# Product of state and C in a Mamba-2 kernel: two products of 64 rows in two banks, one for each half of the heads

The kernel runs on one core of a Trainium2 chip (trn2). The metric is the time of one execution on the device, in microseconds (us), read as the median of several runs.

## The reference, cut to what matters

Four sequences of 768 tokens, 8 heads of width 32, state size 16, go through a chunked state-space layer; its output, 3072 x 256, goes through a feed-forward layer of width 2048. All is fp32.

```python
# per chunk of the sequence (the kernel uses chunks of 128 tokens)
M = einsum('bhin,bhjn->bhij', Cc, Bc) * L          # L: decays, lower triangle
y_intra = einsum('bhij,bhjd->bhid', M, xc)
y_inter = einsum('bhin,bhnd->bhid', Cc, state) * exp(cum)   # the product changed here
y = y_intra + y_inter
state = decay * state + sum_j(Bc x xc * decay_from_j)
...
h = y @ w_in
out = (h * cos(h)) @ w_out
```

## The kernel before

Six chunks of 128 tokens are worked off; in the feed-forward loop of one chunk (16 steps: `hp` = first product, `o` = second) the state-space work of the next chunk is threaded in, one piece in a step: `turn` (transposes), `intra` (C·B products into `g`, times decays into `m`), `finish` (state product and `m`·x into `y`, then the new state's product `s_ps`). Chunk 0 has no state, so 5 chunks x 4 sequences = 20 calls of `finish` hold the state product.

The state of one sequence is kept block-diagonal: partitions are (head, state index) = 8 x 16, columns are (head, width) = 8 x 32, and all but a head's own block is zero. Columns 0 to 127 (heads 0 to 3) are thus non-zero only in rows 0 to 63, columns 128 to 255 only in rows 64 to 127.

```python
def pair(name):                       # two banks, two such tiles in turn
    return psum.tile([P, 2, 4 * P], FP32, tag="scan", bufs=2, name=name)

def finish(c, b, tag=None, fills=0):
    (bcT, m), xr = part.pop((c, b)), raw[c][1]
    y = (pair("y")[:, 0] if tag is None else bank([P, 4 * P], "y", tag)
         ).rearrange("p (k i) -> p k i", k=4)
    fill(y[:, 2:4], fills)
    y = y[:, 0:2]
    if c > 0:
        s = state[c - 1, b].rearrange("p h d -> p (h d)")
        for t in range(2):
            PE.matmul(y[:, t], lhsT=s[:, t * P:(t + 1) * P], rhs=bcT[:, 1],
                      start=(t == 0), stop=False, skip_group_check=True)
    for h in range(H):                                  # y<-m,xr
        q, t = h % 4, h // 4
        PE.matmul(y[32 * q:32 * q + 32, t], lhsT=xr[:, b, h], rhs=m[:, h],
                  start=(c == 0 and t == 0), stop=True, tile_position=(0, 32 * q), ...)
    ...
    ACT.copy(out=yT[c][:, :, b * P:(b + 1) * P], in_=y)
    if c > 0:
        carry(c, b)                                     # s_ps<-xr,sc, 128x32 tiles

def intra(c, b):
    ...
    for u in range(4):                                  # g<-cT,bcT, 32x128 tiles
        r = slice(32 * u, 32 * u + 32)
        PE.matmul(g[u // 2][:, u % 2, 0:2 * P], lhsT=bcT[r, 0], rhs=cT[r]..., ...)
```

Of the kernel before, what the change touches and what calls it, by code (L numbers as in the profile page):

```python
# [25 lines left out]
def kernel(  # L26
# [23 lines left out]
    V, ACT, G, PE = nc.vector, nc.scalar, nc.gpsimd, nc.tensor  # L50
# [3 lines left out]
    P = 128  # L54
# [24 lines left out]
    def bank(shape, name, tag):  # L79
        return psum.tile(shape, FP32, tag=tag, bufs=2, name=name)  # L80

    def pair(name):

        return psum.tile([P, 2, 4 * P], FP32, tag="scan", bufs=2, name=name)
# [6 lines left out]
    def fill(dst, times=1):  # L91

        for _ in range(times):
            PE.matmul(dst, lhsT=ones, rhs=ones.unsqueeze(1).to_broadcast([P, dst.shape[1], P]),  # L94
                      start=True, stop=True, skip_group_check=True)
# [104 lines left out]
    for n in (0, 2, 1, 3, 4, 5):  # L200
# [14 lines left out]
                    fill=0.0, base=0, channel_multiplier=1)  # L215
    G.affine_select(out=own, in_=own, pattern=[[N, H], [0, D]], compare_op=ALU.is_ge,
                    fill=0.0, base=N - 1, channel_multiplier=-1)
# [92 lines left out]

    def finish(c, b, tag=None, fills=0):
        (bcT, m), xr = part.pop((c, b)), raw[c][1]
        y = (pair("y")[:, 0] if tag is None else bank([P, 4 * P], "y", tag)
             ).rearrange("p (k i) -> p k i", k=4)
        fill(y[:, 2:4], fills)
        y = y[:, 0:2]
        if c > 0:
            s = state[c - 1, b].rearrange("p h d -> p (h d)")
            for t in range(2):
                PE.matmul(y[:, t], lhsT=s[:, t * P:(t + 1) * P], rhs=bcT[:, 1],  # L320
                          start=(t == 0), stop=False, skip_group_check=True)
        for h in range(H):
            q, t = h % 4, h // 4
            PE.matmul(y[32 * q:32 * q + 32, t], lhsT=xr[:, b, h], rhs=m[:, h],  # L324
                      start=(c == 0 and t == 0), stop=True, tile_position=(0, 32 * q),
                      skip_group_check=True)
        if b == 0:
            yT[c] = two.tile([P, 2, TB], FP32, tag="yT", name="yT")
        ACT.copy(out=yT[c][:, :, b * P:(b + 1) * P], in_=y)  # L329
        if c > 0:  # L330
            carry(c, b)

    def carry(c, b):

        if c == NC - 1:
            return
        xr, sc = raw[c][1], scaled.pop((c, b))
        s_ps = pair("s_ps")[:, 0, 0:2 * D]
        for q in range(4):
            two_ = slice(2 * q, 2 * q + 2)  # L340
            PE.matmul(s_ps[32 * q:32 * q + 32], lhsT=sc[:, two_].rearrange("p h n -> p (h n)"),  # L341
                      rhs=xr[:, b, two_].rearrange("p h d -> p (h d)"), start=True, stop=True,
                      tile_position=(0, 32 * q), skip_group_check=True)
        state[c, b] = new = states.tile([P, H, D], FP32, tag="state", name="state")
        by_two = "p (k t) d -> p k (t d)"
        V.tensor_tensor(out=new.rearrange(by_two, k=HP),
                        in0=s_ps.unsqueeze(1).to_broadcast([P, HP, 2 * D]),
                        in1=own.rearrange(by_two, k=HP), op=ALU.mult)
        if c > 0:
            V.scalar_tensor_tensor(out=new, in0=state.pop((c - 1, b)),  # L350
                                   scalar=reach[c, b][:, P - 1:P], in1=new,
                                   op0=ALU.mult, op1=ALU.add)
# [59 lines left out]
    decays(0, 2, 1)  # L412
    turn(0, 1)
    finish(0, 0, "o")
    intra(0, 1)
    grade(*order[0])
    spread_a(3, ("o", "h"))
    decays(0, 3, 0)
    decays(0, 3, 1)
    turn(0, 2, "h")  # L420
    finish(0, 1, "o", 1)
    intra(0, 2)
    turn(0, 3, "h")
    grade(*order[2])
    join(*order[0])
    finish(0, 2, "o", 1)
    intra(0, 3)
    grade(*order[1])
# [76 lines left out]
```

## Time and profile before

| | before |
|---|---|
| time, median of 3 runs | 410.0 us (409.17 to 410.1) |
| span of the profiled run | 408.6 us |
| TensorE busy | 401.1 us, 98% |
| VectorE, ScalarE busy | 65%, 43% |
| state product | 80 matmul instructions (40 products, two passes each), 12.2 us "busy" |

TensorE is busy all the way, so the question is what TensorE's own sequence costs.

### The profile page before, as it was taken

The numbers are of one execution on the slowest core, as the hardware profiler recorded it, in microseconds if no ns is written. First come the engines' busy times: TensorE is split into PE (matmuls) and PEld (weight loads), VectorE is DVE, ScalarE is ACT, GpSimd is POOL, SyncE is SP. The second block draws the span as 40 slices with busy tenths as digits, with TensorE's granted clock in tenths as the row PEclk, the third lists the DMA queues.
The fourth block names the chain that finished last, engine by engine and source line by source line (L and its number), as shares of the span: only waits on it lengthen the run. The fifth ranks groups of instructions, "written<-read, shape, count | busy, mean of one in ns | idle before, by whom it ended". The sixth has DMA issues, their size and how long they took to land.

```text
span 408.6 us, 5540 instructions
## 1 busy us (share of the span) xinstructions
PE 401.1 (98%) x2094; PEld 263.1 (64%) x2094; DVE 266.7 (65%) x410; ACT 173.8 (43%) x329; POOL 42.3 (10%) x62
## 2 busy tenths in 40 slices
PE   8999999999999999999999999999999999999995
PEld 6646666666666666666666666666666666666664
DVE  4989999945768754777663677674566664444442
ACT  2476666534343434344334433433434342433332
POOL 2164555400000000000000000000000000000000
PEclk9999999999999999999999999999999999999999
DMA  7999994291111092110164211120100000100001
GB/s 96 327 138 309 390 177 113 62 120 54 51 52 53 0 171 63 53 43 10 51 117 65 70 34 51 53 78 0 53 1 2 0 0 2 51 0 2 0 0 53
DMA packets 105979, 30.28 MB, mean 74 GB/s; under 512 B 75168, under 2 KB 101856, under 8 KB 105952
## 3 DMA queue, kind: packets, MB, share of 16 engines
q1 hardware_dynamic: 105952, 29.92, 30.9%
q8 instruction: 16, 0.26, 0.3%
q14 instruction: 11, 0.09, 0.1%
HBM read 26.57 MB, written 3.34 MB: 73 GB/s over the span
## 4 chain that ended last, share of the span: by engine, by line
PE 97%; ACT 1%; DVE 1%; issue 0%; DVEq 0%
PE hp L361 42%; PE o L385 41%; PE g L302 4%; PE y L324 3%; PE y L320 2%; PE a_ps L251 2%; PE warm L94 1%; PE tp L283 1%; PE tp L284 1%; PE s_ps L341 1%; PE y L94 0%; ACT cT L288 0%; ACT w L372 0%; DVE m L306 0%; DVE gT L374 0%
## 5 line engine op out<-in xcount | busy, mean ns | idle before, releaser
L361 PE MATMUL hp<-yT,w_in 128*128 128x512 f32 x384 | 185.0, 604 | 0.6 <-DVE gT L374 0.6
L385 PEld LDWEIGHTS o<-w_out,gT 128*128 128x128 f32 x768 | 145.9, 190 | 59.9 <-issue 44.0
L385 PE MATMUL o<-w_out,gT 128*128 128x256 f32 x768 | 181.1, 379 | 0.0
L365 ACT ACTIVATE k<-hp 128x512 int32<-128x512 f32 x96 | 57.4, 597 | 127.2 <-PE hp L361 127.1
L374 DVE TENSOR_TENSOR gT<-hp,w 128x512 f32<-128x512 f32 x96 | 66.3, 690 | 65.4 <-ACT w L372 65.4
L367 DVE SCALAR_TENSOR_TENSOR w<-hp,k 128x512 f32<-128x512 f32 x96 | 66.0, 687 | 62.3 <-ACT k L365 60.9
L361 PEld LDWEIGHTS hp<-yT,w_in 128*128 128x128 f32 x384 | 67.8, 190 | 57.7 <-issue 53.7
L372 ACT ACTIVATE w<-w,quarter 128x512 f32<-128x512 f32 x96 | 69.3, 722 | 75.1 <-DVE w L367 75.1
L267 DVE TENSOR_TENSOR_SCAN lam<-arow,unit 128x512 f32<-128x512 f32 x40 | 48.6, 1214 | 0.0
L306 DVE TENSOR_TENSOR m<-g,lam 128x512 f32<-128x512 f32 x48 | 30.7, 681 | 0.7 <-PE g L302 0.6
L276 POOL TENSOR_TENSOR sc<-bc,lam 128x128 f32<-128x128 f32 x20 | 8.2, 412 | 203.0 <-DVE lam L267 200.6
L288 ACT ACTIVATE cT<-tp,slot 128x128 f32<-128x128 f32 x48 | 14.6, 355 | 12.7 <-PE tp L284 12.7
L302 PE MATMUL g<-cT,bcT 32*128 32x256 f32 x192 | 17.1, 426 | 1.2 <-ACT bcT L290 1.2
L324 PE MATMUL y<-m,xr 128*32 128x128 f32 x384 | 15.8, 279 | 0.2 <-DVE m L306 0.2
L191 DVE SCALAR_TENSOR_TENSOR mag<-words,mag 128x512 uint32<-128x512 uint32 x16 | 13.4, 840 | 0.6
L329 ACT COPY yT<-y 128x256 f32<-128x256 f32 x24 | 8.9, 372 | 11.3 <-PE y L324 11.3
L302 PEld LDWEIGHTS g<-cT,bcT 32*128 32x128 f32 x192 | 7.5, 182 | 8.7 <-issue 6.5
L320 PEld LDWEIGHTS y<-bcT,state 128*128 128x128 f32 x80 | 12.1, 191 | 1.0
L171 POOL TENSOR_SCALAR mag<-mag 128x512 f32<-128x512 f32 x16 | 11.7, 731 | 9.4 <-ACT mag L170 9.2
L320 PE MATMUL y<-bcT,state 128*128 128x128 f32 x80 | 12.2, 274 | 0.0
L324 PEld LDWEIGHTS y<-m,xr 128*32 128x32 f32 x384 | 8.9, 109 | 4.3 <-DVE m L306 1.4
L170 ACT ACTIVATE mag<-words 128x512 f32<-128x512 f32 x16 | 10.9, 681 | 0.9 <-DMA words<-in_moe_w_in_dram 0.9
(43 smaller groups left out, 156.0 us busy)
## 6 DMA issues: line engine op xcount, KB each, us to landing
arow<-a_cut SPq DMA_DIRECT2D x20, 512.0 KB
words<-in_moe_w_in_dram SPq DMA_DIRECT2D x8, 512.0 KB
words<-in_moe_w_out_dram SPq DMA_DIRECT2D x8, 512.0 KB
xr<-in_x_dram SPq DMA_DIRECT2D x5, 512.0 KB
out_dram<-ob SPq DMA_DIRECT2D x10, 256.0 KB
bc<-in_B_dram SPq DMA_DIRECT2D x5, 256.0 KB
bc<-in_C_dram SPq DMA_DIRECT2D x5, 256.0 KB
along<-a_all SPq DMA_DIRECT2D x20, 64.0 KB
```

The source lines that it names most:

```text
L267: V.tensor_tensor_scan(out=lam[c, b][:, hs].rearrange("p h i -> p (h i)"), data0=rows_.rearrange("p h i -> p (h i)"), data1=unit.rearrange ...
L288: ACT.activation(cT[:, t], tp[:, 1], AF.Copy, scale=slot[:, t:t + 1])
L302: PE.matmul(g[u // 2][:, u % 2, 0:2 * P], lhsT=bcT[r, 0], rhs=cT[r].rearrange("p t i -> p (t i)"), start=True, stop=True)
L306: V.tensor_tensor(out=m[:, hs].rearrange("p (k t) i -> p k (t i)", k=2), in0=g[u][:, :, 0:2 * P], in1=l[:, hs].rearrange("p (k t) i -> p k ...
L320: PE.matmul(y[:, t], lhsT=s[:, t * P:(t + 1) * P], rhs=bcT[:, 1], start=(t == 0), stop=False, skip_group_check=True)
L324: PE.matmul(y[32 * q:32 * q + 32, t], lhsT=xr[:, b, h], rhs=m[:, h], start=(c == 0 and t == 0), stop=True, tile_position=(0, 32 * q), skip ...
L361: PE.matmul(hp[n], lhsT=w_in[:, k, f * P:(f + 1) * P], rhs=yT[c][:, k], start=(k == 0), stop=(k == KT - 1))
L365: ACT.activation(k, hp[n], AF.Copy, bias=0.25, scale=INV_2PI)
L367: V.scalar_tensor_tensor(out=w, in0=hp[n], scalar=INV_2PI, in1=k, op0=ALU.mult, op1=ALU.subtract)
L372: ACT.activation(cos, cos, AF.Sin, bias=quarter, scale=TWO_PI)
L374: V.tensor_tensor(out=gT[n], in0=hp.pop(n), in1=cos, op=ALU.mult)
L385: PE.matmul(o[c][b // 2][:, b % 2], lhsT=g[:, b * P:(b + 1) * P], rhs=w_out[:, f], start=(f == 0 and (last or b % 2 == 0)), stop=(f == NF ...
```

## The change

Each half of the heads needs only its own 64 rows. The change gives each product those 64 rows (a tile of 64 x 128 in the array) and a bank of its own, so that the two can run at the same time instead of one after the other. The two-bank tile was already allocated; only half of it was in use.

```diff
-        y = (pair("y")[:, 0] if tag is None else bank([P, 4 * P], "y", tag)
-             ).rearrange("p (k i) -> p k i", k=4)
-        fill(y[:, 2:4], fills)
-        y = y[:, 0:2]
         if c > 0:
+            y = pair("y")[:, :, 0:P]
             s = state[c - 1, b].rearrange("p h d -> p (h d)")
             for t in range(2):
-                PE.matmul(y[:, t], lhsT=s[:, t * P:(t + 1) * P], rhs=bcT[:, 1],
-                          start=(t == 0), stop=False, skip_group_check=True)
+                r = slice(t * P // 2, (t + 1) * P // 2)
+                PE.matmul(y[:, t], lhsT=s[r, t * P:(t + 1) * P], rhs=bcT[r, 1],
+                          start=True, stop=False, skip_group_check=True)
+        else:
+            y = bank([P, 4, P], "y", tag)
+            fill(y[:, 2:4], fills)
+            y = y[:, 0:2]
```

## The prediction

> **What bounds the kernel now.** I read the page first, then the groups of PE instructions, then the timeline of PE over one block of the loop. The page's busy line and the chain that ended last say who sets the time:
>
> ```profile
> PE 401.1 (98%) x2094; PEld 263.1 (64%) x2094; DVE 266.7 (65%) x410; ACT 173.8 (43%) x329; POOL 42.3 (10%) x62
> ...
> PE 97%; ACT 1%; DVE 1%; issue 0%; DVEq 0%
> ```
>
> TensorE is busy 98% of 408.6 us and 97% of the last-ending chain is TensorE following itself. DVE, the next, is busy 65%. So a nanosecond taken off TensorE's sequence is a nanosecond off the end, and nothing else counts unless it makes TensorE wait. The changed product is the first of these groups; the other two are the kernel's existing small products, which I use to price it:
>
> ```profile
> L320 PE MATMUL y<-bcT,state 128*128 128x128 f32 x80 | 12.2, 274 | 0.0
> L302 PE MATMUL g<-cT,bcT 32*128 32x256 f32 x192 | 17.1, 426 | 1.2 <-ACT bcT L290 1.2
> L324 PE MATMUL y<-m,xr 128*32 128x128 f32 x384 | 15.8, 279 | 0.2 <-DVE m L306 0.2
> ```
>
> 5 chunks with a state, 4 sequences and 2 products make 40 products; the count is 80, so an fp32 product is two instructions (two passes over the columns). 274 ns of one is its latency, not its price, as they are pipelined: the price has to come from start-to-start times. Those stand in the timeline of PE, where a line merges a run of one kind (start, length to the end of the last, count):
>
> ```profile
> 180.38 1.89 PE L385 MATMUL o<-w_out,gT 128*128 128x256 f32 x8
> 182.20 0.71 PE L302 MATMUL g<-cT,bcT 32*128 32x256 f32 x8
> 182.85 1.98 PE L361 MATMUL hp<-yT,w_in 128*128 128x512 f32 x4
> 184.67 1.89 PE L385 MATMUL o<-w_out,gT 128*128 128x256 f32 x8
> 186.40 0.61 PE L320 MATMUL y<-bcT,state 128*128 128x128 f32 x4
> 186.93 0.65 PE L324 MATMUL y<-m,xr 128*32 128x128 f32 x16
> 187.39 0.29 PE L341 MATMUL s_ps<-xr,sc 128*32 128x64 f32 x8
> 187.62 1.98 PE L361 MATMUL hp<-yT,w_in 128*128 128x512 f32 x4
> 189.44 1.89 PE L385 MATMUL o<-w_out,gT 128*128 128x256 f32 x8
> 191.17 0.27 PE L283 MATMUL tp<-ident,bc 128*128 128x128 f32 x1
> 191.28 0.27 PE L284 MATMUL tp<-ident,bc 128*128 128x128 f32 x1
> 191.38 1.88 PE L361 MATMUL hp<-yT,w_in 128*128 128x512 f32 x4
> 193.10 1.89 PE L385 MATMUL o<-w_out,gT 128*128 128x256 f32 x8
> ```
>
> After the names of what is written and read stands the array's shape (rows*columns), then the moving operand's. Successive starts of o in the records are 216 ns apart (256 columns, one pass), of y<-bcT,state 110 ns (128 columns). From o at 184.67 to y at 186.40 is 1.73 us = 8 x 0.216: full-array work follows full-array work with no gap. But o at 180.38 to g at 182.20 is 1.82, which is 0.093 more. Likewise y<-bcT,state at 186.40 to y<-m,xr at 186.93 is 0.53 = 4 x 0.110 + 0.093. Whenever the shape of the array changes, TensorE stands for some 93 ns, in records that the page still counts as busy.
>
> A second cost follows. hp to o takes 1.72 us where nothing changed before it (191.38 to 193.10) and 1.82 after g or s_ps (182.85 to 184.67, 187.62 to 189.44): 0.10 more, because after a change the first weights cannot be loaded behind running work. For g it shows too: 182.20 to 182.85 is 0.65 = 2 passes x 0.216 + 0.104 for the weights + 0.108 to leave the shape.
>
> **What the Trainium skill says.** "TensorEngine Tiling (Array Packing)", section Key Properties: changing the tiling mode, not just the tile, drains the TensorE. The trace agrees, with 93 ns at each change from full rows to 32-row or 32-column tiles. The same page, Gotcha 1: PSUM Pressure: different row tiles must not write one PSUM bank at once; that is why the changed kernel takes a bank for each product. "TensorE: Matmul & The Clock Gate", Part 3, in its closing advice: a product of few rows takes as long as one of 128 rows, and the gain is that tiles run at once. The trace agrees: in g, four products of 32 rows start 6 to 7 ns apart and the block lasts two passes, not eight. The same page, LDWEIGHTS (loading the stationary operand): the load takes the number of columns divided by 1.2 GHz, whatever the rows; 107 ns for 128. The trace agrees: 104 ns exposed for g's 32 rows as for hp's 128. Halving the rows therefore makes no load shorter.
>
> **The change part by part.** The order of instructions on every engine is the same in the built program, with as many of each; y already took a two-bank tile in this stage, so no buffer gets scarcer; chunk 0 keeps its old form. What changes is 20 blocks (5 chunks x 4 sequences) of TensorE between the last o and the first y<-m,xr. I count each from the start of that last o.
>
> - Before: 216 ns (o streams) + 4 x 110 (two products, two passes each, one after the other) + 95 (change to 32-column tiles) = 751 to 753 ns. All 20 blocks have it within 1 ns.
> - Removed: two of the four 110 ns passes, as both products run at once: -220 ns.
> - Added: a change from full rows to 64-row tiles: +93 ns. Its weights cannot be loaded behind o any more: +104 ns. The second pair starts some 7 ns apart: about +7. The load for the second pass (about 106) fits behind the first (110), so nothing for that.
> - Kept: a change of shape to the 32-column tiles, taken at the 92 that a change from 32-column tiles straight to g's 32-row tiles costs early in the trace (202 ns start to start less the pass of 110).
> - After: 216 + 93 + 104 + 110 + 110 + 7 + 92 = 732 ns, so about 20 ns less, by 20 blocks 0.4 us.
>
> The rest of the block is unchanged: y<-m,xr at two banks for its two halves streams the same columns, and its copy to yT reads the same 256 elements a partition (median 372 ns, on an engine with 43% of its time busy). So 410.0 - 0.4 = 409.6 us. The intended halving of 12.2 us of "busy" is nearly all paid back at the doorway.
>
> **The rivals.**
> - The full gain: no drain and no exposed load, -220 x 20 = 4.4 us, 405.6 us (-1.1%). For it: o is already done with weights by then. Against: all 20 entries into g show the 93 and the 104, and g is also made of row tiles. Chance about 4%.
> - The two products don't overlap fully. If TensorE keeps the order first product both passes, second product both passes, and overlaps only the middle two, one more pass stays: 110 less the 20 = +88 ns a block, 1.8 us, 411.8 us. If they don't overlap at all, +199 ns a block, 4.0 us, 414.0 us (+1.0%). For it: nothing in this trace has two tiles of 64 rows, and the passes of a product follow one another. Against: the eight of g start as four and four, and so do those of y<-m,xr, so TensorE does interleave passes across tiles. Chance 10% together.
> - A wait moves in: if y<-m,xr comes earlier, it may find m not ready. m ended 258 ns ahead of it in the tightest block, over 2.2 us in most; 20 ns use up none of this. An eviction across two banks could hold ACT longer, but it has idle time in every block. Under 2%, and worth tenths of a us.
>
> **Range and chances.** The main sum says -0.4 us with perhaps 0.03 us a block of doubt on the drain of a 64-row shape, 0.6 us; three runs of the kernel before spread over 0.9 us (409.17 to 410.1). Together with the partly overlapped case on the upper side: 408.7 to 411.2. Every rival that I can name stays inside 2% (401.8 to 418.2), so within 2% gets 0.98, and 0.01 each way.
>
> **What would show each step right or wrong.** In the groups of PE, y<-bcT,state should have 64 rows in place of 128, still 80 of them. In the timeline, o to y<-bcT,state should grow from 1.73 to about 1.82 (the drain), and y<-bcT,state to y<-m,xr shrink from 0.53 to about 0.42 (0.104 + 2 x 0.110 + 0.10). If that second stretch is near 0.31, the load was hidden and the gain is real; if near 0.53 (one pass more) or 0.63 (two more), the products did not run at once. Everything from y<-m,xr to the next o should keep its length. PE's total busy time should hardly move, within 1 us of 401.1. I am wrong if the first stretch stays at 1.73, if the copies of yT lengthen and PE gets an idle entry behind them, or if a wait of PE on m or on y's bank shows in the list of waits where there was almost none.

## The result, and the profile after

The changed kernel takes 409.28 us (median of 6 runs, 408.8 to 409.78); the kernel before took 409.9 in 6 runs. The ratio is 0.9985, 95% interval 0.9971 to 0.9999. A ratio here is the mean time of one kernel's fast runs over that of the other's of the same rounds, so it is not quite the ratio of the medians. By the rule used here, under which a difference counts from 2%, the two are the same.

The busy line of the page of the changed kernel, and its group of the state product:

```profile
PE 400.8 (98%) x2094; PEld 257.1 (63%) x2094; DVE 267.0 (65%) x410; ACT 173.6 (43%) x329; POOL 43.5 (11%) x62
```

```profile
L320 PE MATMUL y<-bcT,state 64*128 64x128 f32 x80 | 9.8, 322 | 0.1
```

The product now has 64 rows, still 80 instructions. Its mean record got longer, 322 ns for 274, and its busy time shorter, 9.8 us for 12.2. Both are poor measures: a record counts the wait for its own weights, and two overlapping records count once. TensorE's total fell by 0.3 us, not by 2.4. The block itself stands in the timeline of TensorE of the changed kernel (start, length, count):

```profile
184.67 1.89 PE L389 MATMUL o<-w_out,gT 128*128 128x256 f32 x8
186.49 0.49 PE L320 MATMUL y<-bcT,state 64*128 64x128 f32 x4
186.91 0.64 PE L328 MATMUL y<-m,xr 128*32 128x128 f32 x16
187.37 0.29 PE L345 MATMUL s_ps<-xr,sc 128*32 128x64 f32 x8
187.59 1.98 PE L365 MATMUL hp<-yT,w_in 128*128 128x512 f32 x4
189.41 1.89 PE L389 MATMUL o<-w_out,gT 128*128 128x256 f32 x8
```

o to y<-bcT,state is 1.82 us, where it was 1.73: the change of shape comes before the product now. y<-bcT,state to y<-m,xr is 0.42, where it was 0.53. From there on every distance is what it was. In the records' nanoseconds, from the start of the last o:

| stretch of the block, ns | before | after |
|---|---|---|
| last o to first y<-bcT,state | 216 | 309 |
| first y<-bcT,state to first y<-m,xr | 537 | 422 |
| sum | 753 | 731 |

All 20 blocks of the kernel before have 753 or 754; 19 of the changed kernel's have 730 or 731. The profiled spans, 408.6 and 408.1 us, differ by 0.58 us, and the starts of all pieces in the two traces account for that: 20 blocks give 0.45 us, the first block of the changed kernel lost 0.14 in a wait, 0.06 was lost in the first 10 us (mean granted clock of the run 0.998 against 1.000), and 0.33 came off after the last instruction of TensorE, while the output lands and the program closes. Only the first of these four is the change.

The one wait: in the first block y could not start until DVE had read the bank pair that it reuses (the first half of m). DVE is busiest at that time (9.9 us of the 10 from 40 to 50). The wait is of that run and not of the change. The changed kernel's second profile (after_again, below) has none: its first block is 730 ns. The doubled kernel before (x2_before, below), which has neither the rows nor the second bank of the change, has one of 309 ns. In nine of the twelve profiles the first y starts 54 to 56 ns after that half of m has ended; only those of the kernel before, after_again and t64x32 show no wait. The page's chain of work that ended last tells the two kinds apart. It is 97% TensorE in these three profiles and 88 to 91% in the other nine, as in the changed kernel's:

```profile
PE 88%; SPq 6%; DMA 2%; DVE 2%; issue 1%; ACT 0%
```

At the wait, 44 us into the run, this chain leaves TensorE for DVE. So TensorE's sequence alone sets the time only from there on; that the profile before showed 97% was in part the luck of that run.

A trap is worth showing. The list of waits of the weight loads of the changed kernel has two new entries (engine, line, released by: us in all, times, longest):

```profile
PEld y L320 <- DVE w L371: 5.3, 16, 0.3
PEld y L320 <- DVE m L306: 1.5, 4, 0.5
```

This reads as if all 20 blocks waited for DVE. They did not, but for the longest one of the second entry: the weight load starts 307 or 308 ns after the last o in 19 blocks of 20, exactly as in all 20 groups of g that follow an o, for which the list names ACT or no engine. In the kernel before, the same load starts 1 or 2 ns after the last o, so its data were there. The load is idle through 216 ns of o's stream and 93 ns of drain, and the profile puts idle time down to whatever semaphore came last.

### The profile page after: what moved, and what is told of

It reads as the page before. It is cut to its first block, busy times and chain, and to the rows that moved or that the text cites. A ratio compares the mean times of both kernels' runs of the same rounds, so it can differ in the third digit from the quotient of the medians.

```text
span 408.1 us, 5540 instructions
## 1 busy us (share of the span) xinstructions
PE 400.8 (98%) x2094; PEld 257.1 (63%) x2094; DVE 267.0 (65%) x410; ACT 173.6 (43%) x329; POOL 43.5 (11%) x62
## 4 chain that ended last, share of the span: by engine, by line
PE 88%; SPq 6%; DMA 2%; DVE 2%; issue 1%; ACT 0%
PE hp L365 40%; PE o L389 39%; SPq L112 5%; PE g L302 3%; PE y L328 3%; PE y L320 2%; DMA words<-in_moe_w_in_dram 1%; SPq L129 1%; DMA arow<-a_cut 1%; DVE mag L191 1%; PE tp L283 1%; PE tp L284 1%; PE s_ps L345 0%; DVE w L371 0%; DVE gT L378 0%
## 5 line engine op out<-in xcount | busy, mean ns | idle before, releaser
L171 POOL TENSOR_SCALAR mag<-mag 128x512 f32<-128x512 f32 x16 | 12.8, 802 | 9.0 <-ACT mag L170 9.0
L195 POOL TENSOR_TENSOR w_out<-mag,last 128x512 uint32<-128x512 uint32 x8 | 10.2, 1276 | 8.3 <-DVE mag L191 7.6
L195 POOL TENSOR_TENSOR w_in<-mag,last 128x512 uint32<-128x512 uint32 x8 | 10.3, 1287 | 7.2 <-DVE mag L191 7.2
```

Source lines behind the costliest of these rows:

```text
L195: G.tensor_tensor(out=dst.bitcast(U32), in0=bits.rearrange("p (k f) -> p k f", k=k), in1=last.rearrange("p (k f) -> p k f", k=k), op=ALU.add)
```

## The experiments

Ten runs in all, each with the kernel before on the same chip. The edits are against the changed kernel, except in x2_before and col32, which are edits of the kernel before.

**Half of the change: two banks, all 128 rows.**

```diff
-                r = slice(t * P // 2, (t + 1) * P // 2)
-                PE.matmul(y[:, t], lhsT=s[r, t * P:(t + 1) * P], rhs=bcT[r, 1],
+                PE.matmul(y[:, t], lhsT=s[:, t * P:(t + 1) * P], rhs=bcT[:, 1],
```

> The two products keep all 128 rows and only get a bank each (half of the change). Theory (the time is set by shapes of the array and passes, banks are free): the block from the last o to the first y<-m,xr stays at 753 ns as in the kernel before, 410 us within 0.3. Rival (the second bank itself costs or gains something, for instance in the copy to yT or in the changed accumulation): a block different from 753 ns by more than 5 ns, or copies of yT whose median is not 372 ns.

Block 753 or 754 ns in 19 blocks (the first one waited for its bank pair, as told above), copies of yT 373 ns, ratio 1.0013 (0.9985 to 1.0041). The bank alone does nothing, in either direction. Whether two row tiles need a bank each is not shown: no run put both in one bank.

**Row tiles that cannot overlap.** Both products read rows 0 to 63.

```diff
-                r = slice(t * P // 2, (t + 1) * P // 2)
+                r = slice(0, P // 2)
```

> Both products read rows 0 to 63, so they cannot run at once; the result is wrong on purpose (heads 4 to 7 lose their state term). Theory (the change pays about 200 ns to enter a 64-row shape and gets 220 ns back by running both at once): the block is 309 + 206 + 2 x 110 + 202 = 937 ns instead of 731, so 20 x 206 = 4.1 us over the changed kernel, about 413.4 us. Rival (the 64-row products were cheap for another reason, such as a shorter pass of fewer rows): the block stays near 731 to 800 ns and the time under 411 us.

The timeline of TensorE of this kernel:

```profile
199.65 1.89 PE L389 MATMUL o<-w_out,gT 128*128 128x256 f32 x8
201.47 0.71 PE L320 MATMUL y<-bcT,state 64*128 64x128 f32 x4
202.11 0.64 PE L328 MATMUL y<-m,xr 128*32 128x128 f32 x16
```

The block is 309 + 639 = 948 ns, 217 more than the changed kernel's and 11 more than expected (I had taken 206 ns from the second tile's start to the next pass instead of 214 from the first one's; the rest is passes of 111 rather than 110). The ratio is 1.0098 to the kernel before, 414.21 us. The rival of a cheaper pass for fewer rows falls: a pass of 64 rows costs what one of 128 does. This is also the price of the new shape alone: 948 - 753 = 195 ns with no overlap to set against it.

**The products done twice, before and after.** If the overlap is real and the entry is paid once, more work of the same shape should let the full gain through.

```diff
-            for t in range(2):
+            for t in (0, 1, 0, 1):
```

> The kernel before with each state product done twice over (same result, as each pair starts its sum anew). Theory: four more passes of 110 ns in a block with no change of shape: 753 + 440 = 1193 ns, 20 x 0.44 = 8.8 us more than before, about 418.7 us. Rival (part of these passes lies behind something): less than 7 us more.

> The changed kernel with each state product done twice over. Theory: the entry into the 64-row shape is paid once, and each further pair of products costs two passes of 110 ns, as the halves run at once: 731 + 220 = 951 ns, 4.4 us more than the changed kernel, about 413.7 us, and 1.2% below the doubled kernel before. Rival (the entry is paid for every pair, or the interleaving breaks down with four products in line): a block above 1000 ns and a lead over the doubled kernel before of under 3 us.

First the doubled kernel before, then the doubled changed kernel, both in TensorE's timeline:

```profile
203.24 1.05 PE L320 MATMUL y<-bcT,state 128*128 128x128 f32 x8
204.22 0.65 PE L324 MATMUL y<-m,xr 128*32 128x128 f32 x16
```

```profile
200.91 0.72 PE L320 MATMUL y<-bcT,state 64*128 64x128 f32 x8
201.56 0.64 PE L328 MATMUL y<-m,xr 128*32 128x128 f32 x16
```

With 128 rows, eight instructions take 0.98 us to the next piece; with 64 rows, 0.65. The blocks are 1200 and 954 ns: doubling adds 447 ns to the one and 223 to the other. The times are 418.88 us (ratio 1.0212) and 414.36 us (1.0106), a lead of 4.5 us where the single products led by 0.6. The doubled changed kernel overlaps fully and still pays its entry once. So the small result of the change is not a failed overlap: some 220 ns are gained, and some 200 are spent at the door.

**What the door costs: fewer columns to a tile.** The entry is a drain of 93 ns plus about 100 ns until the first pass streams. If the latter is a weight load, it should go with the columns of the tile. The two products were cut into four tiles of 64 x 64, then eight of 64 x 32; all the pieces have places of their own in the array.

```diff
-                PE.matmul(y[:, t], lhsT=s[r, t * P:(t + 1) * P], rhs=bcT[r, 1],
-                          start=True, stop=False, skip_group_check=True)
+                for v in range(2):                       # range(4), 32 for eight tiles
+                    f, w = t * P + 64 * v, 64
+                    PE.matmul(y[w * v:w * v + w, t], lhsT=s[r, f:f + w], rhs=bcT[r, 1],
+                              start=True, stop=False, tile_position=(64 * t, w * v), ...)
```

> The changed kernel with each product cut once more, into two of 64 columns: four tiles of 64 x 64, all at once. Theory (part of the entry is a weight load that nothing hides, and it goes by the number of columns): the load exposed falls from about 100 ns to about 53, two more starts of 7 ns each come before the last one; the stretch from the first y<-bcT,state to the first y<-m,xr is about 386 ns instead of 422, 20 x 36 = 0.7 us off, about 408.6 us. Rival (the 100 ns are a fixed cost of the new shape, not a load): the stretch stays at 422 or grows by the added starts to about 436.

> The changed kernel with each product cut into four of 32 columns: eight tiles of 64 x 32, all at once. Theory (exposed load by columns): load exposed about 26 ns, six more starts of 7 ns: stretch about 384 ns, as good as four tiles of 64 x 64, about 408.6 us. Rival (fixed cost): 422 plus 42, about 464 ns, and 0.8 us more than the changed kernel.

TensorE's timeline with four tiles, then with eight:

```profile
199.35 0.45 PE L322 MATMUL y<-bcT,state 64*64 64x128 f32 x8
199.73 0.64 PE L331 MATMUL y<-m,xr 128*32 128x128 f32 x16
```

```profile
197.42 0.45 PE L322 MATMUL y<-bcT,state 64*32 64x128 f32 x16
197.79 0.64 PE L331 MATMUL y<-m,xr 128*32 128x128 f32 x16
```

Both stretches are 379 ns, for 422 with two tiles, so the rival of a fixed cost falls. From the first pass to the second of the same tile it takes 213 ns with 128 columns, 160 with 64 and 133 with 32. That is 53 ns less for 64 columns less and 27 for another 32, so in proportion to the columns; carried on to no columns it leaves 107 ns for the pass, and 106, 53 and 26 ns are the exposed load. That the eight tiles gain no more than the four is the starts' doing: the last of four starts 20 ns after the first, the last of eight 47, and 160 + 20 = 133 + 47. The times are 408.85 us (ratio 0.9973, 0.9961 to 0.9986) and 408.86 (0.997, 0.9954 to 0.9985), against 20 x (753 - 688) = 1.3 us under the kernel before worked out from the blocks.

**One change of shape less, and no row tiles.** The state products take the shape of y<-m,xr, eight column tiles of 128 x 32 in one bank.

```diff
-            for t in range(2):
-                PE.matmul(y[:, t], lhsT=s[:, t * P:(t + 1) * P], rhs=bcT[:, 1],
-                          start=(t == 0), stop=False, skip_group_check=True)
+            for h in range(H):
+                q, t = h % 4, h // 4
+                PE.matmul(y[32 * q:32 * q + 32, t], lhsT=s[:, h * D:(h + 1) * D],
+                          rhs=bcT[:, 1], start=(t == 0), stop=False,
+                          tile_position=(0, 32 * q), skip_group_check=True)
```

> The state products with all 128 rows in eight column tiles of 32, the shape of y<-m,xr, in one bank as before: no row tiles, and one change of shape in the block instead of two. Theory: 216 + 93 to enter, then the passes take four groups of 110 ns as in y<-m,xr (371 ns first to last start), and y<-m,xr follows after another 89 with no change: about 769 ns to the first y<-m,xr, whose own entry is then cheaper by the 23 ns of its exposed load, so within 10 ns of the kernel before for the whole block and within 0.3 us of its time. Rival (the change of shape is what costs, and dropping one saves 93 ns or more a block): 1.9 us faster than the kernel before, about 408.1 us.

```profile
197.06 1.89 PE L387 MATMUL o<-w_out,gT 128*128 128x256 f32 x8
198.88 0.64 PE L321 MATMUL y<-bcT,state 128*32 128x128 f32 x16
199.34 0.62 PE L326 MATMUL y<-m,xr 128*32 128x128 f32 x16
```

In this timeline the drain stands in front of the state product (1.82 us from o), and y<-m,xr follows with none: 770 ns to its first start, then 348 ns from its first to its last start instead of 372. From the last o to the next o it is 3253 ns, where the kernel before has 3260. The ratio is 0.9997. The drain was moved, not saved: the kernel before already has just one change on the way into the column tiles, and the changed kernel is the one that adds a second.

**The lesson applied to g as well.** Eight tiles of 64 x 32 for the state product, and g's four tiles of 32 x 128 cut into eight of 32 x 64, since g pays the same exposed load.

```diff
+            for v in range(2):
+                js = slice(64 * v, 64 * v + 64)
-            PE.matmul(g[u // 2][:, u % 2, 0:2 * P], lhsT=bcT[r, 0],
+                PE.matmul(g[u // 2][js, u % 2, 0:2 * P], lhsT=bcT[r, 0, js],
+                          tile_position=(32 * u, 64 * v), ...
```

> The eight tiles of 64 x 32 for the state products, and besides each product of g cut into two of 64 columns (eight tiles of 32 x 64). Theory (exposed load by columns at every entry): g's first to last start falls from 340 to about 318 ns in 24 blocks, 0.5 us on top of the 0.7 of the state products, about 408.1 us. Rival (fixed cost): g grows by 28 ns from the four added starts, and the time is above that of the eight tiles alone.

```profile
181.17 0.69 PE L304 MATMUL g<-cT,bcT 32*64 32x256 f32 x16
181.79 1.98 PE L371 MATMUL hp<-yT,w_in 128*128 128x512 f32 x4
```

g's first to last start is 313 or 314 ns for 340 in 21 of 24 groups (the others start among the waits of the first 45 us), and the step from g to hp 0.62 us in this timeline for 0.65 before. 408.66 us, ratio 0.9963 (0.995 to 0.9976). To compare it with the changed kernel directly, both ran once more on one chip:

> The changed kernel once more, on the chip of the next run, so that the two can be compared. From its block (731 ns against 753): 0.4 us under the kernel before, a ratio of 0.9990 within the noise of about 0.0015.

> The best version so far beside the changed kernel, on one chip. From the blocks of its first run: 20 x (731 - 688) + 24 x (340 - 313) = 0.86 + 0.65 = 1.5 us under the changed kernel and 1.95 us under the kernel before, a ratio of 0.9952 to the kernel before. If the ratio is above that of the changed kernel less 0.0015, the gain seen in its blocks is not reaching the end.

The changed kernel: 409.73 us, ratio 0.9987 (0.9974 to 1.0001). The version with finer tiles: 408.28 us, ratio 0.9951 (0.9938 to 0.9965), against 0.9952 worked out from the blocks. It beats the kernel before by 0.5% and the changed kernel by 0.35%, with a correct result. That is small, but its interval stays clear of 1 and of the changed kernel's.

## Why the prediction was right

- **TensorE's own sequence sets the time.** Held from 44 us on: every experiment moved the time (its ratio times the 410 us of the kernel before) by what its blocks said (x 20, within 0.6 us), from 2.0 us less to 8.7 more. Before that, one wait on DVE can come in.
- **The added drain, +93 ns.** Held: 216 became 309 in 19 of 20 blocks and in every experiment with a tiled entry.
- **The added weight load, +104 ns.** Held, and shown to be a load: 106, 53 and 26 ns for 128, 64 and 32 columns. Rows did not matter: g's tiles of 32 rows and 128 columns expose 104.
- **The removed passes, -220 ns.** Held: serialised on purpose the block is 217 ns longer, and doubling adds 224 ns more to the kernel before than to the changed one.
- **The exit from the new shape at the old price.** Held: 202 ns from the last start to y<-m,xr, for 205 before.
- **The sum.** 732 ns foreseen, 731 measured; 20 blocks make 0.45 us, 409.6 foreseen and 409.28 measured. The measured difference of the medians, 0.6 us, is more than the blocks' 0.45, but the runs cannot tell the two apart. The range had a slip that did no harm: its upper end, 411.2, is said to take in the partly overlapped case, which the prediction itself puts at 411.8.
- **The rivals.** The full gain fell with the first stretch (1.82, not 1.73). Lost or partial overlap fell with the second (0.42, not 0.53 or 0.63). A wait on y's bank did come, once, 0.14 us, in a run where DVE was late. By the letter of the prediction's last sentence that is a sign of being wrong; it was not due to the change and cost 0.03%. I had checked that m was ready in time for y<-m,xr (258 ns), not that y's bank was free in time for the state product's weight load, which comes first and had 104 ns in the profile before.

One of the prediction's signs was empty: TensorE's busy total hardly moved, as foreseen, but that number would have said nothing in any case, since a drain counts as busy.

## What to carry to other kernels

Cutting a small matmul into row tiles that run at once saves streaming time but pays an entry: here 93 ns of drain and a weight load that nothing hides. Count both before cutting; for two passes saved they ate nine tenths of the gain, for four they would have eaten under half. If you enter a tiled shape anyway, cut its columns too until the load is as short as the added starts are long (64 columns here).

## What the Trainium skill lacked or had wrong

- "TensorEngine Tiling (Array Packing)", Key Properties, says that changing the tiling mode drains the array, without a size. Here each change cost 88 to 95 ns, from or to 64-row, 32-row and 32-column tiles (start to start, less the pass); entering a tiled shape also exposed a weight load of 106, 53 or 26 ns for 128, 64 or 32 columns of fp32.
- The same page lists tile sizes and speedups by the factor of tiling. No page has the break-even: two products of 128 columns in fp32 gained 22 ns of 220; done twice, 246 ns of 440.
- "TensorE: Matmul & The Clock Gate", Part 3, gives about 4 ns from the start of one tile's matmul to the next tile's. Here it was 6 to 7 ns in the packed groups that nothing held up, which is why eight tiles were no better than four.
- The same part says that matmuls start strictly in program order. In the built programs an fp32 product's two passes stand one behind the other, product by product; in the records as many passes as there are tiles start 6 to 7 ns apart, and as many again follow together, with two, four and eight tiles alike. The records do not name the tile, but where products stand in line two passes of one are 109 ns apart at the least (kernel before), so passes of later products start before earlier ones.
